# Chunks 0 and 1 of a windowed attention: scores over all 128 rows with zeros beside a head's q, and weighted values over all 128 columns with both heads' v

## The chip, the core and the metric

The kernel runs on one core of one Trainium2 chip. The metric is the device time of one execution in microseconds (us), over a few executions of the same program. Five engines work side by side and wait for one another through semaphores: PE (matrix multiply, with PEld for its weight loads), DVE (vector), ACT (scalar and activation), POOL and SP. SP and ACT also issue the transfers from and to memory. Matmuls read SBUF and write PSUM.

## What is computed

Sliding-window attention with a linear position bias, and behind it a feed-forward layer:

```python
batch, n_heads, seq, head_dim = (8, 8, 576, 64)
...
    window = 128
    scale = 1.0 / np.sqrt(D)
    scores = scale * np.matmul(q, k.transpose(0, 1, 3, 2))
    ...
    bias = slopes[:, None, None] * (-np.abs(rel).astype(np.float32))[None, :, :]
    mask = (rel >= 0) & (rel < window)
    scores = np.where(mask, scores + bias[None], -1000000000.0)
    scores = scores - np.max(scores, axis=-1, keepdims=True)
    attn = np.exp(scores)
    attn = attn / (np.sum(attn, axis=-1, keepdims=True) + 1e-09)
    return np.matmul(attn, v).astype(np.float32)
...
    h = x @ w_in
    g = np.where(pos, h, np.where(neg, 0.0, (h + beta) ** 2 / (4.0 * beta)))
    return (g @ w_out).astype(np.float32)
```

The attention output of 8 heads of 64 makes x of 4608 rows by 512; w_in is 512 by 2048, w_out 2048 by 512. Both weights arrive in 64-bit floats and are converted on the chip.

## The kernel before

**Tiling.** The 4608 tokens are cut into 12 chunks of 384 (`CH`), each of three blocks of 128. A chunk has 8 heads, taken in 4 pairs; the two heads of a pair lie beside each other in the 128 rows of q and k (transposed: row is head dimension, column is token), the even head (j = 0) in rows 0 to 63 and the odd head (j = 1) in rows 64 to 127. Heads are numbered `m` through the whole program (chunk c = m // 8), pairs `p` likewise.

**Stages of a head.** `prepare_q` scales q (L232). `scores` (L264) multiplies, for each of the three blocks, the block's q by up to 256 columns of k into PSUM (tile `s`), DVE adds the bias and takes the row's extremum (L294, tile `z`), ACT exponentiates with a running sum (L296), and DVE divides and folds the two halves of the window into one 128-wide tile `ep` (L302 to L309). `weights_t` (L312) transposes `ep` on PE (L318, tile `p`), ACT copies it out (L321, tile `lu`), and POOL makes a lower and an upper triangle of it (L322, L324). `values` (L337) multiplies v by these triangles into PSUM (tile `x`, L359), and one copy takes the result to `xn`.

**The first two chunks** (`LIGHT = 2`) use plain float32 matmuls, each of which stands in the trace as two PE records; the others use operands split in a high and a low part (L290, L291, L383). In chunks 0 and 1 a score matmul reads the 64 rows of its head alone (`ql[r, 0, qs]`, `kr[r, 0, ks]`, L288), and a value matmul has the 64 columns of its head's v as weights (`vn[:, i + b0, j]`, L359). In chunk 0 the two heads of a pair write the two halves of one PSUM bank, which is copied once for both (L364, DVE for odd pairs, ACT for even ones); in chunk 1 each head has a bank of its own, and is copied alone (L366, L368).

**The feed-forward layer** of a chunk runs over 16 slices of 128 of the inner width (`layer1`, L405 to L419, tiles `h`, `sg`, `g`; `layer2`, L430 to L447, tiles `acc`). Its matmuls are 128 rows by 128 columns: `h` in split form, and in chunk 0 `acc` in plain float32 (L438).

**Order.** Python code writes the attention of chunk c + 1 between the slices of the feed-forward layer of chunk c (`segments`, `emit_attention`). A scheduler then settles each engine's program; an engine runs it strictly in that order. Ahead of the first layer stands the whole attention of chunk 0, and with it the conversion of the first four slices of the weights (`EARLY`, `fetch_weights`, `convert_in`, `convert_out`, L123 to L146) on ACT and DVE; the other twelve are converted during chunk 0's feed-forward layer. Two runs of transposes of the identity (`keep_busy`, L84) stand at the start of PE's program, before and behind the first scores.

Of the kernel before, what the change touches and what calls it, by code (L numbers as in the profile page):

```python
# [8 lines left out]
F32 = mybir.dt.float32  # L9
# [3 lines left out]
AF = mybir.ActivationFunctionType  # L13
# [5 lines left out]
def windowed_attention_then_ffn(  # L19
# [21 lines left out]
    V, S, G, T, DMA = nc.vector, nc.scalar, nc.gpsimd, nc.tensor, nc.sync  # L41

    H, SEQ, D = 8, 576, 64
    NT, DM = out.shape
    DFF = w_in.shape[1]
    P = 128
    NPAIR = H // 2
    NCC = DM // P
    NFC = DFF // P
    NQB = 3  # L50
    CH = NQB * P
# [35 lines left out]

    loaded = const.tile([P, 1], F32, name="loaded")
    S.activation(loaded, quarter, AF.Exp)
    qscale = const.tile([P, NPAIR], F32, name="qscale")  # L90
    for g in range(NPAIR):
        G.memset(qscale[:D, g:g + 1], 4.0 ** g / 4.0)
# [14 lines left out]
    rel_end = const.tile([P, 2 * P], F32, name="rel_end")  # L107
    V.tensor_copy(rel_end, rel)
    V.memset(rel_end[D:, :P + D], NEG)


    wi, wo, wf = [None] * NFC, [None] * NFC, {}
# [68 lines left out]
    def load_first(p):  # L181

        n = f"_{p}"
        if p == 0:
            qq = [ap1.tile([P, CH], F32, name="qr" + n, tag="qr"), ap1.tile([P, 2, CH], F32, name="ql" + n, tag="ql")[:, 0]]
            kv = [ap1.tile([P, CH + P], F32, name="kr" + n, tag="kr")[:, :CH], ap1.tile([P, CH], F32, name="vn" + n, tag="vn")]
        elif p == 1:
            t = ap1.tile([P, 2, CH], F32, name="qq" + n, tag="kl")
            qq = [t[:, 0], t[:, 1]]
            kv = [ap1.tile([P, CH], F32, name="kr" + n, tag="kk"), ap1.tile([P, CH], F32, name="vn" + n, tag="vs")]  # L190
        else:
            t = wp.tile([P, 2, CH], F32, name="qq" + n, tag=f"wi{NFC - NPAIR + p}")
            qq = [t[:, 0], t[:, 1]]
            t = wp.tile([P, 2, CH], F32, name="kv" + n, tag=f"wo{NFC - NPAIR + p}")
            kv = [t[:, 0], t[:, 1]]
        vn = kv[1].rearrange("p (i j d) -> p i j d", j=2, d=D)
        pair[p] = dict(qr=qq[0], ql=qq[1].rearrange("p (o t) -> p o t", o=1), kr=kv[0].rearrange("p (o t) -> p o t", o=1), vn=vn)
        DMA.dma_start(qq[0], q[p * P:(p + 1) * P, :CH])
        DMA.dma_start(kv[0], k[p * P:(p + 1) * P, :CH])
        DMA.dma_start(vn.rearrange("p i j d -> p i (j d)"), v[:CH, p * P:(p + 1) * P].rearrange("(i p) d -> p i d", p=P))  # L200

# [30 lines left out]
    def prepare_q(p):  # L232
        qr = pair[p]["qr"]
        if p // NPAIR < LIGHT:
            if p >= NPAIR:
                pair[p]["ql"] = ap1.tile([P, 2, CH], F32, name=f"ql_{p}", tag="ql")
            return S.activation(pair[p]["ql"][:, 0], qr, AF.Copy, scale=qscale[:, p % NPAIR:p % NPAIR + 1])
        ql = pair[p]["ql"] = ap1.tile([P, 2, CH], F32R, name=f"ql_{p}", tag="ql")
        for j in range(2):
            scale = 2.0 ** (2 * (p % NPAIR) + j + 1) / 8.0  # L240
            o_hi, o_lo, s = ql[lo_rows[j], j], ql[hi_rows[j], j], qr[lo_rows[j]]
            S.mul(o_hi, s, scale)
            V.scalar_tensor_tensor(o_lo, s, scale, o_hi.bitcast(F32), ALU.mult, ALU.subtract)
# [20 lines left out]
    def scores(m, blks):  # L264
# [15 lines left out]
        for n, i in enumerate(blks):  # L280
            lone = i + b0 == 0
            c0 = P if lone else D if c % CYCLE == 1 and i == 2 else 0
            k0 = (i + b0 - 1) * P + c0
            o = pt[:, n, c0:]
            win.append((o, c0, lone))
            if c < LIGHT:
                r, qs, ks = lo_rows[j], slice(i * P, (i + 1) * P), slice(k0, k0 + 2 * P - c0)
                st["scored"] = T.matmul(o, ql[r, 0, qs], kr[r, 0, ks], start=True, stop=True).ins  # L288
                continue
            T.matmul(o, ql[:, j, i * P:(i + 1) * P], kk[:, j, k0:k0 + 2 * P - c0], start=True, stop=False)  # L290
            T.matmul(o, ql[:, j, i * P:(i + 1) * P], kl[:, j, k0:k0 + 2 * P - c0], start=False, stop=True)  # L291
# [45 lines left out]
    def values(m):  # L337
        p, j = divmod(m, 2)
        c, g = divmod(p, NPAIR)
        vn, vs, lu = pair[p]["vn"], pair[p].get("vs"), head[m]["lu"]  # L340
        b0 = before(c)
        if j == 0:
            xn[c, g] = xp1.tile([P, CH], F32, name=f"xn_{c}_{g}", tag=f"xn{g}")
        if c == 0:

            if j == 0:
                pair[p]["px"] = ps_acc.tile([P, DM], F32, name=f"x_{m}", tag="acc")
            pb = pair[p]["px"]
        else:
            pb = bank(f"x_{m}")  # L350
        px, pf = pb[:, :CH], pb.rearrange("r (i w) -> r i w", w=P)
        o = xn[c, g][lo_rows[j]]
        if c < LIGHT:
            po = px[lo_rows[j]] if c == 0 else px[:D]
            todo = [i for i in (0, 1, 2, -1) if i + b0 >= 0]
            for n, i in enumerate(todo):
                q0, q1 = max(i, 0), min(i + 2, NQB)
                first = 2 * i + 1 if i >= 0 else 0
                last_x[0] = T.matmul(po[:, q0 * P:q1 * P], vn[:, i + b0, j],  # L359
                         lu[:, 0, first:first + q1 - q0, :].bitcast(F32).rearrange("p a w -> p (a w)"),  # L360
                         start=(n == 0), stop=(n == len(todo) - 1), skip_group_check=True).ins
            if c == 0:
                if j:
                    (V.tensor_copy if g % 2 else S.copy)(xn[c, g], px)  # L364
            elif j:
                S.copy(o, po)  # L366
            else:
                V.tensor_copy(o, po)  # L368
            del head[m]
            if j == 1:  # L370
                del pair[p]
            return
        alone = -1 if b0 else NQB - 1
        todo = [(i, s) for i in range(-b0, NQB) if i != alone for s in range(2)] + [(alone, 0)]
        for n, (i, s) in enumerate(todo):
            w = vs[:, i + b0, j].rearrange("p s d -> p (s d)")
            q0, q1 = max(i, 0), min(i + 2, NQB)
            first = 2 * i + 1 if i >= 0 else 0
            if i == alone:
                ox, lx = pf[:, q0::NQB - q0, :], lu[:, :, first, :]  # L380
            else:
                ox, lx = px[:, q0 * P:q1 * P], lu[:, s, first:first + q1 - q0, :].rearrange("p a w -> p (a w)")
            T.matmul(ox, w, lx, start=(n == 0), stop=(n == len(todo) - 1), skip_group_check=True)  # L383
        S.copy(o, px[D:, :])
        V.tensor_tensor(o, px[:D, :], o, ALU.add)
        o = o[:, q0 * P:(q0 + 1) * P]
        V.tensor_tensor(o, pf[:D, NQB, :], o, ALU.add)
        del head[m]
        if j == 1:
            del pair[p]  # L390
# [187 lines left out]
```

## Time and profile before

| what | value |
|---|---|
| median of 3 executions | 1060.94 us (1060.28 to 1061.31) |
| the profiled execution's own time | 1068.07 us |
| its span, first to last instruction | 1066.0 us |
| mean granted PE clock | 0.981 |
| PE busy | 97% |
| DVE, ACT, POOL busy | 74%, 58%, 35% |
| first matmul of the first layer | 53.86 us |

The page gives each engine's busy time, then the span in 40 slices (digits are tenths; the row PEclk is the clock that PE was granted), the chain of work that ended last, and the costliest groups of instructions. Other views of the same trace are a table by stretches of time (busy time of each engine, granted clock, transfers), the timeline of one engine, and the chain in order of time. In these, "x6" behind a group of plain float32 matmuls means six records, so three matmuls. PE counts as busy while a matmul is in flight, so 100% does not say that it runs at full clock.

### The profile page before, as it was taken

The numbers are of one execution on the slowest core, as the hardware profiler recorded it, in microseconds if no ns is written. First come the engines' busy times: TensorE is split into PE (matmuls) and PEld (weight loads), VectorE is DVE, ScalarE is ACT, GpSimd is POOL, SyncE is SP. The second block draws the span as 40 slices with busy tenths as digits, with TensorE's granted clock in tenths as the row PEclk, the third lists the DMA queues.
The fourth block names the chain that finished last, engine by engine and source line by source line (L and its number), as shares of the span: only waits on it lengthen the run. The fifth ranks groups of instructions, "written<-read, shape, count | busy, mean of one in ns | idle before, by whom it ended". The sixth has DMA issues, their size and how long they took to land.

```text
span 1066.0 us, 16843 instructions
## 1 busy us (share of the span) xinstructions
PE 1038.2 (97%) x5508; PEld 906.8 (85%) x5508; DVE 790.1 (74%) x2249; ACT 618.9 (58%) x1476; POOL 369.2 (35%) x419
## 2 busy tenths in 40 slices
PE   8999999999999999999999999999999999999998
PEld 5576667998988988998998988999889889899996
DVE  6687799878877788877678887777787897863322
ACT  6687766656556556656456565555555655742322
POOL 2120004444443433433343443433333443333221
PEclk8599999999999999999999999999999999999999
DMA  8346412112212122121113112111121221200000
GB/s 284 100 164 202 136 48 67 53 40 67 65 38 67 48 65 67 41 53 60 36 48 89 43 48 65 62 30 38 60 65 38 77 65 48 67 1 1 31 1 30
DMA packets 58903, 69.50 MB, mean 65 GB/s; under 512 B 4032, under 2 KB 44480, under 8 KB 58816
## 3 DMA queue, kind: packets, MB, share of 16 engines
q1 hardware_dynamic: 48064, 51.66, 17.4%
q10 hardware_dynamic: 10752, 16.78, 4.6%
q8 instruction: 43, 0.70, 0.3%
q14 instruction: 44, 0.36, 0.1%
HBM read 58.98 MB, written 9.44 MB: 64 GB/s over the span
## 4 chain that ended last, share of the span: by engine, by line
PE 85%; DVE 6%; ACT 5%; POOL 2%; issue 2%; DMA 0%; ACTq 0%; SPq 0%; DVEq 0%; POOLq 0%
PE h L408 11%; PE h L409 11%; PE h L410 11%; PE acc L441 11%; PE acc L442 10%; PE acc L443 10%; PE x L383 5%; PE acc L438 3%; PE p L318 3%; PE s L291 2%; PE s L290 2%; PE x L359 2%; PE s L288 2%; ACT z L296 1%; POOL lu L333 1%
## 5 line engine op out<-in xcount | busy, mean ns | idle before, releaser
L427 POOL TENSOR_TENSOR gl<-g,gh 128x384 fp32r<-128x384 f32 x176 | 183.5, 1042 | 435.0 <-ACT gh L426 429.1
L408 PE MATMUL h<-xh,wi 128*128 128x384 f32 x768 | 264.8, 345 | 1.7 <-ACT sg L417 1.7
L409 PE MATMUL h<-xl,wi 128*128 128x384 f32 x768 | 259.8, 338 | 0.0
L410 PE MATMUL h<-xh,wi 128*128 128x384 f32 x768 | 259.4, 338 | 0.0
L441 PE MATMUL acc<-wo,gh 128*128 128x512 f32 x528 | 212.0, 401 | 8.1 <-ACT gh L426 8.1
L418 DVE SCALAR_TENSOR_TENSOR g<-sg 128x384 f32<-128x384 f32 x192 | 108.6, 566 | 148.4 <-ACT sg L417 136.4
L442 PE MATMUL acc<-wo,gh 128*128 128x512 f32 x528 | 208.2, 394 | 0.0
L426 ACT CAST gh<-g 128x384 fp32r<-128x384 f32 x176 | 90.3, 513 | 193.6 <-DVE g L419 179.4
L417 ACT ACTIVATE sg<-h,quarter 128x384 f32<-128x384 f32 x192 | 111.2, 579 | 140.2 <-PE h L410 139.5
L296 ACT ACTIVATE z<-z,nmax 128x256 f32<-128x256 f32 (+2 forms) x288 | 139.0, 485 | 28.5 <-DVE nmax L294 26.6
L443 PE MATMUL acc<-wo,gl 128*128 128x512 f32 x528 | 155.5, 398 | 0.0
L408 PEld LDWEIGHTS h<-xh,wi 128*128 128x128 f32 x768 | 144.6, 188 | 10.7 <-ACT sg L417 3.4
L409 PEld LDWEIGHTS h<-xl,wi 128*128 128x128 f32 x768 | 144.6, 188 | 5.9 <-issue 1.4
L410 PEld LDWEIGHTS h<-xh,wi 128*128 128x128 f32 x768 | 144.4, 188 | 0.0
L294 DVE CUSTOM_DVE_ANT_0 z<-s,rel 128x256 f32<-128x256 f32 (+2 forms) x256 | 94.4, 394 | 51.5 <-PE s L291 44.3
L309 DVE CUSTOM_DVE_ANT_0 ep<-z,rc 128x128 f32<-128x128 f32 x256 | 129.9, 548 | 1.6
L331 POOL TENSOR_SCALAR_AFFINE_SELECT lu<-lu 128x768 fp32r<-128x768 f32 x80 | 80.8, 1010 | 130.2 <-DVE lu L329 121.6
L441 PEld LDWEIGHTS acc<-wo,gh 128*128 128x128 f32 x528 | 99.4, 188 | 27.2 <-ACT gh L426 10.6
L419 DVE SCALAR_TENSOR_TENSOR g<-sg,g 128x384 f32<-128x384 f32 x192 | 112.0, 584 | 3.7
L443 PEld LDWEIGHTS acc<-wo,gl 128*128 128x128 f32 x528 | 97.1, 189 | 19.8 <-POOL gl L427 0.2
L442 PEld LDWEIGHTS acc<-wo,gh 128*128 128x128 f32 x528 | 99.5, 188 | 16.5
L333 POOL TENSOR_SCALAR_AFFINE_SELECT lu<-lu 128x768 fp32r<-128x768 f32 x80 | 81.4, 1018 | 4.6
(88 smaller groups left out, 1461.1 us busy)
## 6 DMA issues: line engine op xcount, KB each, us to landing
kr<-in_k_dram SPq DMA_DIRECT2D x60, 256.0 KB, 4.1
out_dram<-o SPq DMA_DIRECT2D x36, 256.0 KB, 2.4
qr<-in_q_dram SPq DMA_DIRECT2D x45, 192.0 KB, 3.7
rawi<-in_moe_w_in_dram ACTq DMA_DIRECT2D x16, 512.0 KB, 4.6
rawo<-in_moe_w_out_dram ACTq DMA_DIRECT2D x16, 512.0 KB, 5.6
vn<-in_v_dram SPq DMA_DIRECT2D x32, 256.0 KB, 2.8
kr<-in_k_dram SPq DMA_DIRECT2D x26, 192.0 KB, 3.4
vn<-in_v_dram SPq DMA_DIRECT2D x14, 192.0 KB, 2.5
```

The lines of the kernel that those rows point to most:

```text
L296: S.activation(z[:, i, c0:], z[:, i, c0:], AF.Exp, bias=nmax[:, i:i + 1], scale=-1.0, accum_out=sm[:, i, 0:1])
L309: st["folded"] = V.tensor_tensor_reduce(out=ep[:, i, :], in0=z[:, i, :P], in1=z[:, i, P:], op0=ALU.add, op1=ALU.add, scale=rc[:, i:i + 1], ...
L408: T.matmul(ph, wi[fc][:, 0, cc, :], xh, start=(cc == 0), stop=False)
L409: T.matmul(ph, wi[fc][:, 0, cc, :], xl, start=False, stop=False)
L410: T.matmul(ph, wi[fc][:, 1, cc, :], xh, start=False, stop=(cc == NCC - 1))
L417: first = S.activation(sg, ph, AF.Relu, bias=quarter[:, 0:1], scale=0.25)
L418: V.scalar_tensor_tensor(g, sg, 0.5, sg, ALU.min, ALU.mult)
L419: last = V.scalar_tensor_tensor(g, sg, -0.25, g, ALU.add, ALU.max)
L427: G.tensor_tensor(gl, g, gh.bitcast(F32), ALU.subtract)
L441: T.matmul(a, gh[:, ts], wo[fc][:, 0], start=first, stop=False)
L442: T.matmul(a, gh[:, ts], wo[fc][:, 1], start=False, stop=False)
L443: T.matmul(a, gl[:, ts], wo[fc][:, 0], start=False, stop=last)
```

## The change

The edit touches only chunks 0 and 1.

- **Scores.** A tile `qz` holds q of a pair twice, 128 rows by 2 by 384: in plane j only the rows of head j carry q, and the other 64 rows are zero. The score matmul of head j reads all 128 rows of plane j and of k. The zeros are set once: those of `qz[0]` by two fills on DVE, those of the other three tiles by six fills on POOL. Pair 0 and the four pairs of chunk 1 use `qz[0]`, pairs 1 to 3 of chunk 0 the others, which lie in the buffers of weight slices 9 to 11 before these are loaded.
- **q.** `prepare_q` scales each head's 64 rows by an instruction of its own: two on ACT for a pair where there was one.
- **Values.** The weights of a value matmul are both heads' v, 128 columns. Its result has the wanted head in that head's 64 rows, and the product with the other head's v in the others, which nothing reads. In chunk 0 each head now has a PSUM bank of its own, as in chunk 1.
- **Copies out.** Each head's 64 rows are copied alone: j = 0 on DVE, j = 1 on ACT. In chunk 0 that makes eight copies of 64 rows where there were four of 128; in chunk 1 their number and engines stay.

```diff
+    qz = [ap1.tile([P, 2, CH], F32, name=f"qz_{p}", tag="ql") if p == 0 else
+          wp.tile([P, 2, CH], F32, name=f"qz_{p}", tag=f"wi{NFC - 4 - p}") for p in range(NPAIR)]
+    V.memset(qz[0][D:, 0], 0.0)
+    V.memset(qz[0][:D, 1], 0.0)
...
+    for t in qz[1:]:
+        G.memset(t[D:, 0], 0.0)
+        G.memset(t[:D, 1], 0.0)
...
-            qq = [ap1.tile([P, CH], F32, name="qr" + n, tag="qr"), ap1.tile([P, 2, CH], F32, name="ql" + n, tag="ql")[:, 0]]
+            qq = ap1.tile([P, CH], F32, name="qr" + n, tag="qr")
...
-        pair[p] = dict(qr=qq[0], ql=qq[1].rearrange("p (o t) -> p o t", o=1), kr=kv[0].rearrange("p (o t) -> p o t", o=1), vn=vn)
-        DMA.dma_start(qq[0], q[p * P:(p + 1) * P, :CH])
+        pair[p] = dict(qr=qq, ql=qz[p], kr=kv[0].rearrange("p (o t) -> p o t", o=1), vn=vn)
+        DMA.dma_start(qq, q[p * P:(p + 1) * P, :CH])
...
-            if p >= NPAIR:
-                pair[p]["ql"] = ap1.tile([P, 2, CH], F32, name=f"ql_{p}", tag="ql")
-            return S.activation(pair[p]["ql"][:, 0], qr, AF.Copy, scale=qscale[:, p % NPAIR:p % NPAIR + 1])
+            pair[p]["ql"] = qz[p if p < NPAIR else 0]
+            for j in range(2):
+                r = lo_rows[j]
+                o = S.activation(pair[p]["ql"][r, j], qr[r], AF.Copy, scale=qscale[r, p % NPAIR:p % NPAIR + 1])
+            return o
...
-                r, qs, ks = lo_rows[j], slice(i * P, (i + 1) * P), slice(k0, k0 + 2 * P - c0)
-                st["scored"] = T.matmul(o, ql[r, 0, qs], kr[r, 0, ks], start=True, stop=True).ins
+                qs, ks = slice(i * P, (i + 1) * P), slice(k0, k0 + 2 * P - c0)
+
+                st["scored"] = T.matmul(o, ql[:, j, qs], kr[:, 0, ks], start=True, stop=True).ins
...
-            if j == 0:
-                pair[p]["px"] = ps_acc.tile([P, DM], F32, name=f"x_{m}", tag="acc")
-            pb = pair[p]["px"]
+            pb = ps_acc.tile([P, DM], F32, name=f"x_{m}", tag="acc")
...
-                last_x[0] = T.matmul(po[:, q0 * P:q1 * P], vn[:, i + b0, j],
+                last_x[0] = T.matmul(px[:, q0 * P:q1 * P], vn[:, i + b0].rearrange("p j d -> p (j d)"),
...
-            if c == 0:
-                if j:
-                    (V.tensor_copy if g % 2 else S.copy)(xn[c, g], px)
-            elif j:
-                S.copy(o, po)
-            else:
-                V.tensor_copy(o, po)
+            (S.copy if j else V.tensor_copy)(o, px[lo_rows[j]])
```

The scheduler orders the first 200 us or so anew. Three places show it; in the names, the number behind a tile's letter is only its buffer's.

PE, the first values of chunk 0 (`x`, heads 0 and 1), before. The sizes are those of the output.

```order
L288 MATMUL s_0_281<-kr_138,qq_137 128x128
L288 MATMUL s_0_281<-kr_138,qq_137 128x256
L288 MATMUL s_2_288<-kr_138,qq_137 128x256
L359 MATMUL x_274<-lu_221,vn_133 64x256 x2
L359 MATMUL x_274<-lu_221,vn_133 64x128
L359 MATMUL x_274<-lu_253,vn_133 64x256 x2
L359 MATMUL x_274<-lu_253,vn_133 64x128
L318 MATMUL p_300<-ident,ep_233 128x128 x3
```

The same place now:

```order
L298 MATMUL s_0_295<-kr_149,qz_93 128x128
L298 MATMUL s_0_295<-kr_149,qz_93 128x256
L298 MATMUL s_2_302<-kr_149,qz_93 128x256
L367 MATMUL x_287<-lu_234,vn_144 128x256 x2
L367 MATMUL x_287<-lu_234,vn_144 128x128
L328 MATMUL p_315<-ident,ep_246 128x128 x3
L367 MATMUL x_340<-lu_266,vn_144 128x256 x2
L367 MATMUL x_340<-lu_266,vn_144 128x128
```

The two heads' values wrote two halves of one bank one right behind the other; now each writes 128 rows of its own bank, and the transposes of head 2 stand between them.

ACT, from the first q to the exponentials of head 0, before:

```order
L237 ACTIVATE ql_131<-qr_130,qscale 128x384
L133 DMA rawi_154<-in_moe_w_in_dram 128x4x256
L139 DMA rawo_156<-in_moe_w_out_dram 128x1024
L237 ACTIVATE qq_137<-qq_137,qscale 128x384
L296 ACTIVATE z_159,sums<-z_159,nmax_160 128x128
L296 ACTIVATE z_159,sums<-z_159,nmax_160 128x256 x2
```

The same place now:

```order
L245 ACTIVATE qz_92<-qr_142,qscale 64x384 x2
L142 DMA rawi_166<-in_moe_w_in_dram 128x4x256
L148 DMA rawo_168<-in_moe_w_out_dram 128x1024
L245 ACTIVATE qz_93<-qr_148,qscale 64x384 x2
L306 ACTIVATE z_171,sums<-z_171,nmax_172 128x128
L306 ACTIVATE z_171,sums<-z_171,nmax_172 128x256 x2
```

Two instructions of 64 rows stand where one of 128 stood, for pair 0 and for pair 1, and the exponentials of head 0 stand behind both.

POOL, from the table of distances (`reli`, from which `rel`, the bias of every score, is cut) to the first triangle, before:

```order
L97 IOTA reli 128x256
L105 MEMSET sums 128x12
L99 AFFINE_SELECT rel<-rel 128x256
L101 AFFINE_SELECT rel<-rel 128x256
L322 AFFINE_SELECT lu_221<-lu_221 128x3x128
```

The same place now:

```order
L102 IOTA reli 128x256
L110 MEMSET sums 128x12
L117 MEMSET qz_93 64x384
L118 MEMSET qz_93 64x384
L117 MEMSET qz_94 64x384
L118 MEMSET qz_94 64x384
L117 MEMSET qz_95 64x384
L118 MEMSET qz_95 64x384
L104 AFFINE_SELECT rel<-rel 128x256
L106 AFFINE_SELECT rel<-rel 128x256
```

The six fills stand ahead of the two cuts of `rel`, which the first bias on DVE waits for.

More of the change, by code (lines that the diff above doesn't have):

```diff
@@ L184, in load_first @@
         if p == 0:
-            qq = [ap1.tile([P, CH], F32, name="qr" + n, tag="qr"), ap1.tile([P, 2, CH], F32, name="ql" + n, tag="ql")[:, 0]]
+            qq = ap1.tile([P, CH], F32, name="qr" + n, tag="qr")
             kv = [ap1.tile([P, CH + P], F32, name="kr" + n, tag="kr")[:, :CH], ap1.tile([P, CH], F32, name="vn" + n, tag="vn")]
         elif p == 1:
-            t = ap1.tile([P, 2, CH], F32, name="qq" + n, tag="kl")
-            qq = [t[:, 0], t[:, 1]]
+            qq = ap1.tile([P, CH], F32, name="qr" + n, tag="kl")
             kv = [ap1.tile([P, CH], F32, name="kr" + n, tag="kk"), ap1.tile([P, CH], F32, name="vn" + n, tag="vs")]
         else:
-            t = wp.tile([P, 2, CH], F32, name="qq" + n, tag=f"wi{NFC - NPAIR + p}")
-            qq = [t[:, 0], t[:, 1]]
+            qq = wp.tile([P, CH], F32, name="qr" + n, tag=f"wi{NFC - NPAIR + p}")
             t = wp.tile([P, 2, CH], F32, name="kv" + n, tag=f"wo{NFC - NPAIR + p}")
@@ L353, in values @@
         if c < LIGHT:
-            po = px[lo_rows[j]] if c == 0 else px[:D]
             todo = [i for i in (0, 1, 2, -1) if i + b0 >= 0]
```

## The prediction

> **What bounds the kernel now.** I read the page first: the busy times (share of the span, instructions) and the granted clock in 40 slices.
>
> ```profile
> PE 1038.2 (97%) x5508; PEld 906.8 (85%) x5508; DVE 790.1 (74%) x2249; ACT 618.9 (58%) x1476; POOL 369.2 (35%) x419
> PEclk8599999999999999999999999999999999999999
> ```
>
> PE is the bound, 97% busy. The one thing out of line is the digit 5 in the second slice (26.7 to 53.3 us): PE had half its clock there, though that is the attention of chunk 0, with work waiting. So the table by stretches comes next (columns: stretch, length, busy us and count on PE, PEld, DVE, ACT, POOL, granted clock, DMA share, GB/s).
>
> ```profile
> 16.00:20.00 4.00, 4.00 (x18) 2.44 (x18) 3.44 (x18) 2.83 (x10) 0.00 (x0) 0.59 1.05 383
> 20.00:24.00 4.00, 4.00 (x19) 2.36 (x19) 3.11 (x14) 3.93 (x10) 1.04 (x2) 1.00 0.99 305
> 24.00:30.00 6.00, 2.79 (x9) 1.33 (x7) 4.42 (x12) 5.34 (x18) 1.43 (x2) 0.68 0.14 54
> 30.00:40.00 10.00, 9.79 (x26) 6.19 (x27) 7.68 (x37) 6.05 (x19) 2.25 (x5) 0.50 0.46 151
> 40.00:52.50 12.50, 12.50 (x34) 7.28 (x33) 6.49 (x33) 6.49 (x17) 2.47 (x5) 0.50 0.25 69
> 52.50:54.00 1.50, 1.50 (x7) 0.84 (x6) 0.24 (x2) 1.50 (x8) 0.03 (x1) 0.69 0.94 359
> 54.00:74.00 20.00, 19.85 (x90) 13.86 (x91) 16.57 (x63) 16.63 (x42) 3.81 (x9) 1.00 0.46 153
> 74.00:129.00 55.00, 55.00 (x232) 36.74 (x231) 43.15 (x118) 41.16 (x84) 6.77 (x13) 1.00 0.56 183
> 129.00:149.00 20.00, 20.00 (x85) 14.21 (x85) 18.05 (x45) 12.50 (x25) 0.00 (x0) 1.00 0.11 27
> 149.00:178.00 29.00, 25.37 (x126) 20.01 (x125) 28.39 (x71) 21.27 (x51) 10.42 (x9) 1.00 0.31 87
> ```
>
> Four stages with four limits. From 20 to 30 us ACT sets the pace (3.93 of 4, 5.34 of 6). From 30 to 54 PE alone is full, at clock 0.50, while DVE and ACT are about half busy. From 54 to 149 PE is full at clock 1.00. From 149 to 178 DVE is (28.39 of 29). From 40 to 52.5 PE is 100% busy and yet not sped up; from 54 on it is 100% busy and is. What differs is what it runs: before 54, matmuls of 64 rows or 64 columns and some transposes; after it, mostly 128 by 128. PE's timeline (start, us, engine, line, out<-in, rows*columns of the array, count) says the same twice.
>
> ```profile
> 1.65 3.25 PE L84 MATMUL idle<-ident 128*128 128x128 f32 x14 [1.65 <-POOL qscale L92]
> 6.80 2.40 PE L84 MATMUL idle<-ident 128*128 128x128 f32 x20
> 15.98 3.31 PE L359 MATMUL x<-lu,vn 128*64 128x256 f32 x12
> 36.74 2.39 PE L359 MATMUL x<-lu,kv 128*64 128x256 f32 x6
> ```
>
> The first 14 full-width transposes take 0.23 us each, the later 20 take 0.12: full-width work brought the clock up, and it was work on the identity, nearly all zeros. And 12 records of two heads' values in 3.31 us, where 6 of one head take 2.39, means that two halves of the array ran side by side; behind them the clock goes from 0.59 to 1.00. I read from this that the grant follows how much of the array is in use, and that zeros count.
>
> **The change, part by part.** *Clock in 30 to 54 us.* The groups of PE from 30 to 54:
>
> ```profile
> L359 PE MATMUL x<-lu,kv 128*64 128x256 f32 x16 | 7.7, 639 | 0.0
> L318 PE MATMUL p<-ident,ep 128*128 128x128 f32 x15 | 5.0, 446 | 1.3 <-DVE ep L307 1.3
> L288 PE MATMUL s<-kr,ql 64*128 64x256 f32 x8 | 4.1, 671 | 0.0
> L288 PE MATMUL s<-kv,qq 64*128 64x256 f32 x8 | 3.8, 631 | 0.0
> L359 PE MATMUL x<-lu,kv 128*64 128x128 f32 x8 | 2.3, 384 | 0.0
> L288 PE MATMUL s<-kr,ql 64*128 64x192 f32 x4 | 1.7, 524 | 0.0
> L288 PE MATMUL s<-kv,qq 64*128 64x128 f32 x4 | 1.6, 498 | 0.0
> ```
>
> Count times output width is 12,416 columns. The rate at full clock and full width is read from the first layers, in the chain in order of time (start, us, what):
>
> ```profile
> 53.93 0.37 PE h L408
> 76.39 1.38 PE s L288 x6
> 80.08 2.57 PE acc L438 x6
> 82.66 0.33 PE p L318 x3
> 82.98 1.45 PE x L359 x8
> 90.75 0.48 PE p L318 x3
> 123.58 0.37 PE h L408
> 142.97 0.17 PE h L408
> ```
>
> Six `acc` records of 512 columns in 2.57 us are 0.837 ns a column, and `p` with 128-column weights agrees (0.11 us for 128). So PE needs 12,416 x 0.837 ns = 10.4 us where it now takes 23.7 (9.79, 12.50 and the 1.4 up to the first `h` at 53.9). Then ACT and DVE are late next. ACT has 6.05 + 6.49 + 1.5 = 14.0 us of work there, and gets more:
>
> ```profile
> L242 ACT ACTIVATE ql<-qr 64x384 fp32r<-64x384 f32 x2 | 1.0, 522 | 0.0
> L237 ACT ACTIVATE qq<-qq,qscale 128x384 f32<-128x384 f32 x3 | 1.8, 613 | 2.7 <-DMA qq<-in_q_dram 2.7
> L366 ACT COPY xn<-x 64x384 f32<-64x384 f32 x4 | 1.9, 472 | 0.1
> L364 ACT COPY xn<-x 128x384 f32<-128x384 f32 x2 | 1.0, 479 | 3.3 <-PE x L359 3.3
> L368 DVE COPY xn<-x 64x384 f32<-64x384 f32 x4 | 2.2, 541 | 0.0
> ```
>
> 64 rows cost what 128 do (0.472 against 0.479; 0.522 against 0.613), so each second half of a q is about 0.52 us more, and each copy more is 0.47 on ACT or 0.54 on DVE: in all 8 x 0.52 + 2 x 0.47 = 5.1 us on ACT and 2 x 0.54 = 1.1 on DVE. Three q halves and one copy of these fall in this stretch: 14.0 + 2.0 = 16.0 us. DVE has 7.68 + 6.49 + 0.24 + 0.5 = 14.9. The gain is at most 23.7 - 16.0 = 7.7 and at least nothing. ACT where it set the pace was 89% busy (24 to 30 us); at that share 16.0 us of work last 18.0: **-5.7 us**.
>
> *The first 30 us.* Two q halves now stand ahead of head 0's first exponential, and six fills ahead of the cuts of `rel` on POOL:
>
> ```profile
> 7.24 1.47 ACT z L296 x6
> 3.14 0.40 POOL L99 TENSOR_SCALAR_AFFINE_SELECT rel<-rel 128x256 f32<-128x256 f32 x1 [0.35 <-DVE rel L98]
> L300 POOL MEMSET z<- 128x64 f32 x2 | 0.3, 154 | 1.8 <-DVE rc L309 1.8
> masks.py:197 POOL MEMSET ident<- 128x128 f32 x1 | 0.2, 205 | 0.3 <-POOLq L559 0.3
> ```
>
> By 154 and 205 ns for 64 and 128 columns a fill of 384 is 0.41 us, six are 2.5: the cuts start at 5.6 instead of 3.14 and end, at 0.40 each, near 6.5. The first bias, which needs them, goes ahead of the exponential at 7.24, so they cost 0 to 0.9 us, beside the q half's 0.5, which comes at the same moment. The doubled scores and the pair of values at half clock (13.6 to 19.3 us) would save up to 2.5 us at full clock, but ACT sets the pace right behind them and has two more q halves, 1.0 us, to do there. I take **+0.5 us**, with ends at -2.0 and +0.9. DVE's two fills of `qz[0]` stand in time in which DVE waits for `reli`.
>
> *Borders between shapes, 54 to 124 us.* Six `s` records of 1408 columns should take 1.18 us and take 1.38; eight `x` of 1536 should take 1.29 and take 1.45; the first `h` behind either takes 0.37, behind `acc` 0.17; `p` behind `x` takes 0.48, behind `acc` 0.33. So each border between 64 and 128 costs the piece behind it 0.15 to 0.20 us, and `acc` to `h`, which also changes the number format but not the shape, costs nothing. PE's timeline has 30 such borders from the first `h` at 53.9 to that at 123.6: 10 into `h`, 8 into `s`, 8 into `x`, 4 into `p`, in all 2.0 + 1.6 + 1.3 + 0.6 = 5.5 us, on the engine that is full. At full width there are none. Of these, 12 lie before 74, where ACT (16.63 of 20) and DVE are nearly full and ACT gets the last two q halves; I count those at half: **-4.4 us**, with ends at 0 and -5.5.
>
> From 149 on I cost nothing: DVE, full from there to 178, has 3.4 + 11.9 + 2.0 = 17 us of slack from 54 to 149, so it can come there earlier with PE. Without that cover, everything is lost there.
>
> The sum is -5.7 + 0.5 - 4.4 = -9.6 us on the profiled execution's 1068.1, so 1058.5. Its time is 7.1 us above the median of the runs, 1060.9; the difference carries over, and the forecast is **1051.3 us**.
>
> **The rivals.** *B: the clock stays at half.* The rows bear it out as far as 22 us of full PE did not raise it; against it stand the 12 side-by-side records and the identity transposes. PE then needs 12,416 x 1.67 = 20.8 us instead of 23.7 (the borders go), but the pair of values at 16 us, no longer side by side, takes 2 x 2.14 instead of 3.31, 1.0 more: -2.9 + 1.0 + 0.5 - 4.4 = -5.8, **1055.1 us**. The Trainium skill, "TensorE: Matmul & The Clock Gate", Part 1, says that the gate opens after a window of some 3.4 us in which PE is busy; if busy means occupied, width changes nothing and this rival holds, but by that reading the stretch from 40 to 52.5 should already run at 1.00, and its row says 0.50. The same page's Part 3 speaks against the change: matmuls on different strips of the array run concurrently, which full width gives up; the row of 12 in 3.31 us agrees, and the 1.0 us above is its price at half clock.
>
> *C: DVE takes it back.* If DVE cannot come to 149 us earlier, PE waits there for all it gained: **1060.9 us**, give or take 2. For it speaks 28.39 of 29, against it the 17 us of slack.
>
> *D: slower, by ACT's queue.* The 5.1 us of new ACT work lengthen the run where ACT has no idle time left, if also the clock stays and the border cost belongs to the plain float32 weights rather than to shape: +5.1 + 1.0 = **1067.0 us**. It decides once ACT's idle time from 30 to 54 (24 - 14 = 10 us) is under the 2.0 added there. Against it stands that margin, and that `acc`, float32 too, costs no border.
>
> **How the numbers follow.** Forecast 0.62, B 0.21, C 0.10, D 0.07. The best ends (-7.7 - 2.0 - 5.5 = -15.2) give 1045.7; the forecast's poor ends (clock up for half the stretch, -2.9, +0.9, -2.2) 1056.7; B with nothing from 54 to 124 would be 1059.5. The range 1045.5 to 1059 leaves out D and most of C. Within 0.2%, about what a measurement of this kernel can tell from no change, is 1058.8 to 1063.1: C, 0.09. Faster: forecast, B and a little of C, 0.84; slower: 0.07.
>
> **What would show it.** PEclk in the second slice 8 or 9 instead of 5 (B: 5 stays). The first `h` on PE near 48 us instead of 53.9. `s` x6 at 1.18, `x` x8 at 1.29, and `h` behind them at 0.17. ACT some 85 to 90% busy from 30 us to the first `h`. PE's idle time from the first layer's end to 30 us later unchanged at about 3.6 us (C: larger by what was gained). The forecast is wrong if the clock falls back whenever PE, now faster, idles between heads, or if ACT and DVE wait for each other head by head so that the chain and not their work sets that stage.

## The result, and the profile after

| | before | after |
|---|---|---|
| median of 9 executions each | 1060.94 us (1060.28 to 1068.2) | 1055.85 us (1055.16 to 1058.7) |
| ratio | | 0.9943, 95% interval 0.9922 to 0.9965 |
| the profiled execution's own time, mean granted PE clock | 1068.07 us, 0.981 | 1055.43 us, 0.996 |

The kernel became faster by 5.1 us between the medians (0.48%; the ratio, taken over all nine runs of each, is 0.57%): inside the range, 4.5 us above the forecast of 1051.3. Between the two profiled executions the difference is 12.6 us, which is more than the 9.6 forecast for them. Both misses have to be explained.

The page of the changed kernel, its busy times and granted clock in 40 slices:

```profile
PE 1019.9 (97%) x5508; PEld 907.5 (86%) x5508; DVE 792.8 (75%) x2253; ACT 625.7 (59%) x1486; POOL 372.0 (35%) x425
PEclk9999999999999999999999999999999999999999
```

PE runs as many instructions as before (5508) in 18.3 us less, and no slice stands at half clock. The table by stretches (stretch, length, busy us and count on PE, PEld, DVE, ACT, POOL, granted clock, DMA share, GB/s) shows where the time went and what limits now:

```profile
20.00:24.00 4.00, 2.18 (x13) 1.78 (x11) 3.86 (x16) 3.93 (x11) 0.52 (x1) 1.00 1.09 371
24.00:30.00 6.00, 4.09 (x15) 3.33 (x16) 4.26 (x18) 5.93 (x16) 1.27 (x2) 0.76 0.33 102
27.15:30.56 3.41, 3.33 (x13) 2.81 (x12) 2.44 (x14) 3.35 (x10) 0.00 (x0) 0.50 0.26 77
30.56:44.00 13.44, 10.31 (x54) 8.13 (x52) 12.10 (x52) 12.74 (x36) 5.15 (x10) 1.00 0.43 133
44.00:54.00 10.00, 7.38 (x41) 6.24 (x40) 7.47 (x29) 8.44 (x23) 3.29 (x5) 1.00 0.46 164
54.00:74.00 20.00, 20.00 (x92) 15.09 (x91) 18.40 (x65) 18.70 (x42) 3.06 (x7) 1.00 0.59 198
74.00:129.00 55.00, 55.00 (x243) 41.09 (x242) 46.75 (x115) 42.95 (x86) 5.38 (x10) 1.00 0.50 162
136.60:166.60 30.00, 26.73 (x137) 21.49 (x136) 29.53 (x75) 21.24 (x50) 10.07 (x9) 1.00 0.30 84
```

Chunk 0's attention, which PE filled at half clock, is now set by ACT: 5.93 of 6.00 and 12.74 of 13.44 busy, PE idle for a quarter of the time. From 44 to 54 PE, ACT and DVE wait for one another (none is over 85%). From 54 on PE is full, and the stretch that DVE bounds (149 to 178 before) has moved to about 137 to 167, with DVE at 29.53 of 30.

PE's timeline (start, us, engine, line, out<-in, rows*columns, count, idle time before it and what ended that) has the places:

```profile
25.83 1.35 PE L367 MATMUL x<-lu,vn 128*128 128x256 f32 x6 [3.65 <-POOL lu L334]
27.27 0.47 PE L328 MATMUL p<-ident,ep 128*128 128x128 f32 x1
27.53 2.34 PE L298 MATMUL s<-kv,qz 128*128 128x128 f32 x6
35.56 1.35 PE L367 MATMUL x<-lu,kv 128*128 128x256 f32 x6 [1.90 <-POOL lu L334]
44.00 0.42 PE L410 MATMUL h<-xh,wi 128*128 128x384 f32 x1
48.11 0.33 PE L328 MATMUL p<-ident,ep 128*128 128x128 f32 x1 [1.11 <-DVE rc L319]
53.38 0.44 PE L410 MATMUL h<-xh,wi 128*128 128x384 f32 x1 [1.51 <-ACT sg L419]
58.28 1.47 PE L367 MATMUL x<-lu,vn 128*128 128x256 f32 x8
```

The transpose at 27.27, ahead of six `s` records, is the one that stood at 30.21 before: 2.9 us are won by then. The first `h` starts at 44.00 instead of 53.86: 9.9 us. Against before, the twelfth first-layer slice (the `h` at 127.88 before, 116.39 now) is 11.5 us earlier, the sixteenth (148.44 and 136.64) 11.8, and the last of all (1054.15 and 1041.69) 12.5. So four fifths of the difference between the two profiles have arisen by the first `h`, and nothing is lost behind.

### The profile page after: what moved, and what is told of

Its sections match the earlier page's. It is cut to its first block, busy times and chain, and to the rows that moved or that the text cites. A ratio compares the mean times of both kernels' runs of the same rounds, so it can differ in the third digit from the quotient of the medians.

```text
span 1053.6 us, 16864 instructions
## 1 busy us (share of the span) xinstructions
PE 1019.9 (97%) x5508; PEld 907.5 (86%) x5508; DVE 792.8 (75%) x2253; ACT 625.7 (59%) x1486; POOL 372.0 (35%) x425
## 4 chain that ended last, share of the span: by engine, by line
PE 79%; DVE 9%; ACT 7%; issue 3%; POOL 2%; DMA 0%; ACTq 0%; SPq 0%; DVEq 0%; POOLq 0%
PE h L410 11%; PE h L411 11%; PE h L412 11%; PE acc L443 10%; PE acc L444 10%; PE acc L445 10%; PE x L385 5%; PE acc L440 3%; PE p L328 2%; PE s L301 2%; PE s L300 2%; ACT z L306 2%; DVE ep L319 1%; DVE z L304 1%; POOL lu L343 1%
## 5 line engine op out<-in xcount | busy, mean ns | idle before, releaser
L341 POOL TENSOR_SCALAR_AFFINE_SELECT lu<-lu 128x768 fp32r<-128x768 f32 x80 | 80.8, 1010 | 127.3 <-DVE lu L339 117.8
L445 PEld LDWEIGHTS acc<-wo,gl 128*128 128x128 f32 x528 | 97.1, 188 | 19.8
L385 PEld LDWEIGHTS x<-lu,vs 128*128 128x128 f32 x512 | 70.5, 188 | 15.9 <-POOL lu L343 12.2
```

What stands on the lines that cost most here:

```text
L445: T.matmul(a, gl[:, ts], wo[fc][:, 0], start=False, stop=last)
```

## The experiments

Every run has a mean granted PE clock beside its time. The time depends on it: beside the experiments the kernel before ran 88 times (10 as a kernel of its own), from 1059.5 to 1068.3 us, and its 20 runs at a clock of 0.992 have a median of 1060.75, the 14 at 0.981 one of 1067.90. That is 7.15 us for 0.011, or **0.65 us for each 0.001**. 0.001 of a span of 1060 us is 2.1 us at half clock, so a microsecond at half clock costs 0.3. Below, "at a like clock" compares runs of the same mean clock; this is rough, since the mean does not say where in the program the clock was low, and the runs beside 1 to 4, 5 to 8 and 9 to 12 come from three chips. The kernel before's own 11 runs at 0.989 lie between 1061.6 and 1063.5 us, so a difference of a microsecond between a few runs says little.

**1. The kernel before, unchanged.**

> The kernel before, unchanged, profiled and timed again. Theory (the clock's grant in chunk 0's attention differs from run to run, and the profile on which the prediction was made was an unlucky one): the runs spread over several us, the time falls as the granted clock rises, runs near 1061 us have a mean clock near 0.988 to 0.990, runs near 1066 to 1068 have 0.981 to 0.984, and a profile near 1061 shows less than 27 us at half clock before 54 us. Rival (a profiled execution is 7 us longer than a timed one, whatever the clock): all timed runs near 1061 us with the clock at 0.981, and this profile's own time near 1068.

Measured: 1064.73 us (1060.56 to 1068.13), ratio 1.0006 [0.9981, 1.0031]. The profiled execution took 1064.13 us at 0.988, within what the other nine took at their clocks (0.979 to 0.991). It stood at half clock for 17.1 us from 25.7 on, where the first profile did for 27.3 from 26.1; its first `h` started at 48.91 instead of 53.86, 4.95 us earlier, and every later slice up to 576 us by 4.9 to 5.1. Behind one more window of 3.4 us at half clock at 660 us, which the first profile has not, the lead is 3.9 to the end: such a window, where PE is full, costs 1.2. So the 7.1 us that the first profile lay above the median are no cost of profiling: that execution was one of those with the most half clock, and the program itself has no fixed length. Nor does this second profile have the half clock that the first had from 12.5 to 19.3 us.

**2. and 3. One chunk alone.** Chunk 0 alone (scores and values of chunk 1 as before):

```diff
+                if c:
+                    r = lo_rows[j]
+                    st["scored"] = T.matmul(o, ql[r, 0, qs], kr[r, 0, ks], start=True, stop=True).ins
+                    continue
                 st["scored"] = T.matmul(o, ql[:, j, qs], kr[:, 0, ks], start=True, stop=True).ins
...
+                last_x[0] = T.matmul(px[:D, q0 * P:q1 * P] if c else px[:, q0 * P:q1 * P],
+                         vn[:, i + b0, j] if c else vn[:, i + b0].rearrange("p j d -> p (j d)"),
```

> Only chunk 0 has full-width scores and values; chunk 1 is as before. Theory (two separate gains, clock in chunk 0, borders in chunk 1): clock 0.994 to 0.997, the first layer's first matmul near 44 us, time 2 to 4 us under the kernel before, so about 1057.5 to 1058.5. Rival (all of the gain is the clock): the whole 5 us, about 1056.

Chunk 1 alone is the mirror of it, chunk 0 being that of the kernel before.

> Only chunk 1 has full-width scores and values; chunk 0 is as before. Theory: the clock in chunk 0's attention as in the kernel before (mean 0.981 to 0.990, and it may spread), the 30 borders of 0.15 to 0.20 us gone from chunk 0's feed-forward layer, time 2 to 4 us under the kernel before in runs of like clock. Rival (what ACT, DVE and the order do there takes the borders back): within 1 us of the kernel before.

Measured, chunk 0 alone: 1061.65 us (1057.1 to 1065.84), ratio 0.9972 [0.9946, 0.9999], clocks 0.988 to 0.998, the first `h` at 48.36 in its profile: both expectations were missed. At a like clock it is slower than the kernel before: 1061.65 against 1060.75 at 0.992, 1065.22 against 1063.0 at 0.989. Chunk 1 alone: 1056.05 us (1054.43 to 1057.12, four runs), ratio 0.9913 [0.9879, 0.9947], clocks 0.991 to 0.994; at 0.993 it took 1056.05 where the kernel before took 1059.70, so 3.6 us less. What follows, as far as a like mean clock tells: all of the gain at a like clock is chunk 1's, where no border between array shapes is left, and chunk 0's half costs 1 to 2 us; what chunk 0's half gives is clock (0.992 in the mean of these ten runs, 0.988 in the 88).

The trace of chunk 0 alone shows this within one run, in windows of its own:

```profile
25.79:29.20 3.41, 3.41 (x11) 2.95 (x12) 2.18 (x12) 3.36 (x12) 0.00 (x0) 0.50 0.09 36
36.03:39.44 3.41, 3.41 (x11) 2.53 (x10) 1.78 (x10) 1.56 (x4) 0.16 (x1) 0.50 0.14 47
39.44:42.86 3.42, 3.42 (x11) 2.34 (x10) 1.52 (x7) 1.80 (x5) 1.29 (x3) 0.50 0.03 5
46.27:49.68 3.41, 3.41 (x12) 3.05 (x12) 3.06 (x15) 0.90 (x3) 0.16 (x1) 0.50 0.31 95
```

In each of the four PE is busy throughout at half clock. The first holds only full-size matmuls (chunk 0's), and the clock is full behind it. The next two are filled to 57% and 64% by 64-row scores and 64-column values (chunk 1's), and half clock goes on, as it does behind the window from 42.86, with 38%; the last holds only full-size matmuls again, and behind it the clock is full.

**4. Values alone on all columns** (scores, and q in one activation, as before; the copies out as in the changed kernel):

```diff
-            if j == 0:
-                pair[p]["px"] = ps_acc.tile([P, DM], F32, name=f"x_{m}", tag="acc")
-            pb = pair[p]["px"]
+            pb = ps_acc.tile([P, DM], F32, name=f"x_{m}", tag="acc")
...
-                last_x[0] = T.matmul(po[:, q0 * P:q1 * P], vn[:, i + b0, j],
+                last_x[0] = T.matmul(px[:, q0 * P:q1 * P], vn[:, i + b0].rearrange("p j d -> p (j d)"),
```

> Values over all 128 columns in both chunks, scores on a head's 64 rows as before (so no second q halves and no zeros). Theory (the grant follows how much of the array is in use over a few us): full-width values and transposes are enough to lift it, so little time at half clock, mean 0.990 or more; about half of the borders stay; with no second q halves on ACT, which is the bound of chunk 0's attention now, the time is 3 to 6 us under the kernel before. Rival (only all-full-width work lifts the clock): half clock through most of 30 to 50 us, mean 0.981 to 0.988, gain under 2 us.

Measured: 1063.69 us (1060.69 to 1066.2), ratio 0.9992 [0.9971, 1.0012], clocks 0.983 to 0.990: no gain, and a clock as low as before, as the rival had it. Full columns in the values alone do not hold the clock. At a like clock it is 1.0 to 2.2 us under the kernel before (1061.97 against 1063.0 at 0.989, 1063.21 against 1064.97 at 0.987): part of the borders is gone, and ACT has no second q halves.

**5. and 6. Idle transposes in PE's wait**, in the kernel before and in the changed one:

```diff
         emit_attention(turned[m])
+        if t == 4:
+            behind([last_x[0]], lambda: keep_busy(24))
```

> The kernel before, untouched but for 24 idle 128x128 transposes that PE gets behind the values of head 2, where it waits for POOL's triangle from about 24 to 27 us. Theory (the granted clock falls because PE idles in that wait, and half clock costs about 0.3 us per us): no fall at 26 us, mean clock 0.992 to 0.995 in every run, times 1058.5 to 1061, and a median 2 to 4 us under the kernel before of the same call. Rival (64-row scores can't hold the full clock, whatever stands in that wait): the clock falls a few us later all the same, mean clock 0.982 to 0.990 in most runs, 1061 to 1068, the same as before. Second rival (the 2.6 us of transposes end after the triangle is there): +0.5 to +1.5 us at a like clock.

> The changed kernel with the same 24 idle transposes behind the values of head 2. Theory (what is left of its half clock, 3.4 us at 27 us, comes from PE's wait of 3.65 us for POOL's triangle): no half clock after 22 us, mean clock 0.997 or more in every run, times 1054 to 1055.5, the spread of 3.5 us between its runs gone. Rival (the fall is set elsewhere): clock 0.992 to 0.997 and 1055 to 1058.7 as without them. If the transposes outlast the wait: +0.5 us.

Measured, in the kernel before: 1062.71 us (1058.95 to 1073.56), ratio 1.0014 [0.9981, 1.0046], clocks 0.981 to 0.997. In the profiled run (0.997) the half clock from 26 us is gone, as the theory has it, and the time, 1058.95, is lower than any of the 88; but eight of the other nine runs had 0.993 or less, and at a like clock the transposes and the order that the scheduler made around them cost 2 us and more (1062.71 against 1060.75 at 0.992, one run of 1073.56 against 1067.90 at 0.981). In the changed kernel: 1057.69 us (1053.97 to 1060.17), ratio 0.9943 [0.9919, 0.9968]; three runs at 0.998 took 1054.0 to 1054.5, the other seven 1056.2 to 1060.2 at 0.992 to 0.994. Its profile still has a stretch of half clock, at 31.5 us, behind the next wait. So in these profiles PE's wait goes with the fall of the clock, but there is more than one such wait, and filling one only moved the fall in the second. The theories' medians were missed; the rivals came nearer.

**7. q in two activations of 64 rows**, all else as before:

```diff
-            return S.activation(pair[p]["ql"][:, 0], qr, AF.Copy, scale=qscale[:, p % NPAIR:p % NPAIR + 1])
+            for r in lo_rows:
+                o = S.activation(pair[p]["ql"][r, 0], qr[r], AF.Copy, scale=qscale[r, p % NPAIR:p % NPAIR + 1])
+            return o
```

> The kernel before, with each pair's scaled q of chunks 0 and 1 written in two 64-row activations in place of one of 128 rows; matmuls, copies and layout as before. Theory (the about 2 us at a like clock that chunk 0 alone cost over the kernel before are ACT's extra activations): 1.0 to 2.0 us above the kernel before at a like clock (1060.5 to 1061.5 at 0.993, 1064 to 1065 at 0.989). Rival (they come from the separate banks and copies of the values, or from the order): at a like clock within 0.5 us of the kernel before (1059.5 at 0.993, 1063.1 at 0.989).

Measured: 1067.15 us (1062.18 to 1072.26), ratio 1.0033 [1.0007, 1.006], clocks 0.978 to 0.991. At a like clock 0.2 us above the kernel before at 0.988, 0.5 at 0.987, 1.2 at 0.990, 1.6 at 0.991 and 3.5 at 0.986: above it throughout, but scattered over the theory and the rival both. What was not expected is that the clock falls too. The edit alone costs 4 us at the median (0.33% by the ratio).

**8. and 12. The q halves of pairs 2 to 7 on POOL**, in the changed kernel, twice:

```diff
-                o = S.activation(pair[p]["ql"][r, j], qr[r], AF.Copy, scale=qscale[r, p % NPAIR:p % NPAIR + 1])
+                if p < 2:
+                    o = S.activation(pair[p]["ql"][r, j], qr[r], AF.Copy, scale=qscale[r, p % NPAIR:p % NPAIR + 1])
+                else:
+                    o = G.tensor_scalar(pair[p]["ql"][r, j], qr[r], 4.0 ** (p % NPAIR) * (0.5 if j else 0.25), None, ALU.mult)
...
-        behind(done_t[2 * p - 3][1:2] if 2 <= p <= NPAIR + 1 else [], lambda: prepare_q(p))
+        behind(done_t[2 * p - 3][2:3] if 2 <= p < 2 * NPAIR else [], lambda: prepare_q(p))
```

> The changed kernel with the q halves of pairs 2 to 7 written by POOL, each behind the triangles of the head that it stood behind on ACT; those of pairs 0 and 1 stay on ACT. Theory (ACT bounds chunk 0's attention, 97% busy from 16 to 48 us): four activations of 0.47 us leave its queue ahead of the first h, which starts at about 42.5 instead of 44.0, and the time is 1053.5 to 1055. Rival (POOL's triangles are what heads wait for, and the scaling delays them or lengthens the q's own wait): 1056 to 1058, the first h at 44 or later. If both engines are tied head by head: 1055 to 1056.

> The changed kernel with the q halves of pairs 2 to 7 on POOL again, beside the changed kernel. Theory (the 3 us that it was faster than the changed kernel at a clock of 0.992, 1055.3 to 1055.7 against 1058.7, are ACT's four activations in chunk 0 and those of chunk 1): 1053.5 to 1056, and 2 to 3 us under the changed kernel at any like clock; at 0.995 or more 1053 to 1054.5. Rival (like clocks by the span's mean hide where the falls lie, and the two are the same): within 1 us of the changed kernel's median and of its times at a like clock.

Measured: 1055.55 us (1054.46 to 1055.72), ratio 0.9920 [0.9890, 0.9951], and 1055.02 us (1054.3 to 1055.91), ratio 0.9927 [0.9902, 0.9952]. The groups of POOL and the timeline of PE in the first of them:

```profile
L248 POOL TENSOR_SCALAR qz<-qr 64x384 f32<-64x384 f32 x10 | 13.4, 1341 | 0.6
```

```profile
42.52 0.42 PE L413 MATMUL h<-xh,wi 128*128 128x384 f32 x1
```

A half takes POOL 1.34 us, over twice what ACT needs, and still the first `h` starts at 42.5, as expected, because ACT was what chunk 0 waited for. The first set's median lies just above the 1053.5 to 1055 of the theory. At a like clock of 0.992 the two sets took 1055.34 (5 runs) where the changed kernel took 1058.55 (2 runs), at 0.995 1054.46 (5) against 1056.11 (2). But the medians are within 1 us of the changed kernel's: part of it went back in clock. The same trace, far behind:

```profile
316.40:320.95 4.55, 2.05 (x13) 1.53 (x11) 4.36 (x8) 3.53 (x11) 2.66 (x2) 1.00 0.18 38
320.95:324.36 3.41, 2.92 (x10) 2.54 (x11) 3.38 (x14) 1.55 (x5) 1.15 (x2) 0.50 1.02 358
324.36:327.78 3.42, 3.42 (x21) 3.24 (x20) 2.60 (x9) 1.72 (x6) 1.13 (x1) 1.00 0.16 40
```

PE is busy for 2.05 of 4.55 us, then has half clock for 3.41, then full clock again. In the changed kernel's two profiles the clock did not fall there. Faster than the changed kernel by more than the intervals it is not.

**9. The changed kernel again**, beside 10, 11 and 12.

> The changed kernel again, beside the kernel before and the three below. Theory (its gain is about 5 us of clock and about 1 us at a like clock): median 1055 to 1057, mean clock 0.992 to 0.997, ratio 0.992 to 0.996. Rival (the gain was a draw of clocks that another set would not repeat): median 1058 or more with clocks under 0.992 in half of the runs.

Measured: 1055.73 us (1055.41 to 1058.4), ratio 0.9942 [0.9924, 0.996], clocks 0.992 to 0.997, as in the first set. The gain was no draw.

**10. Scores alone on all rows**, with the values on 64 columns as before:

```diff
-                last_x[0] = T.matmul(px[:, q0 * P:q1 * P], vn[:, i + b0].rearrange("p j d -> p (j d)"),
+                last_x[0] = T.matmul(po[:, q0 * P:q1 * P], vn[:, i + b0, j],
```

> Chunks 0 and 1 with scores on all rows and q halves as in the changed kernel, but the values on 64 columns as before. Theory (it is work that fills rows and columns alike that lets the clock stay full, and the borders are gone only where scores and values both have one shape): mean clock 0.984 to 0.990, a median of 1061 to 1066, and at a like clock 1 to 2 us above the kernel before (q halves, no border gone). Rival (rows alone do it, since values alone did not): mean clock 0.992 to 0.997, median 1056 to 1060.

Measured: 1062.82 us (1058.91 to 1064.21), ratio 0.9998 [0.9976, 1.002], nine runs at 0.988 to 0.990 and one at 0.997. As with the values alone, the half measure gives nothing; at a like clock it is within a microsecond of the kernel before (1062.45 against 1063.0 at 0.989, or against 1061.8 in the same set), not 1 to 2 us above it.

**11. Chunk 1 alone with its q halves on POOL**, the edit of 8 applied to the kernel of 3.

> Chunk 0 as in the kernel before; chunk 1 on the full array as in the changed kernel, with its q halves written by POOL behind the triangles. Theory (chunk 1's borders are worth 3.6 us at a like clock, and ACT's four q halves cost chunk 1 up to 1.5 us of it): 1053 to 1056, 1 to 2 us under the 1056.05 that chunk 1 alone gave with its q halves on ACT, 4 to 5 us under the kernel before at a like clock. Rival (in chunk 1 the q halves lie in ACT's idle time): 1055.5 to 1057, nothing gained.

Measured: 1060.78 us (1057.24 to 1062.47), ratio 0.9974 [0.9954, 0.9993], clocks 0.984 to 0.991. At a like clock it is 3.9 us under the kernel before at 0.989, 4.4 at 0.987 and 5.4 at 0.985, as expected, but the clock was as low as in the kernel before, which has the same chunk 0, so the 1053 to 1056 of the theory was missed. The one run at 0.991 took 1057.24, that of experiment 3 at 0.991 took 1057.12: by these two single runs nothing is gained over ACT, the rival. It also warns of experiment 3: its four runs had clocks that ten runs of a kernel with the same chunk 0 hardly reached, so its median of 1056.05 may be a lucky draw.

The clock by kernel: where all of chunk 0 was on the full array, the mean over the runs was 0.995 (changed kernel, 19 runs), 0.995 (6), 0.993 (8 and 12) and 0.992 (2); where it was not, 0.988 (kernel before, 88 runs), 0.986 (4), 0.990 (5), 0.986 (7), 0.990 (10), 0.987 (11), and 0.993 in the four runs of 3.

## Why the prediction was right, and where it was not

**The forecast's mechanisms are the ones that acted**; two terms came out larger between the two profiles, partly because the first profile of the kernel before was of an execution with much half clock, and the last step, from the profiled execution to the median, failed. The time alone would not have shown the mechanism: 1055.85 lies 0.75 us from rival B's 1055.1 and 4.5 from the forecast. What decides against B is the granted clock in the traces.

*Clock in 30 to 54 us, forecast -5.7.* From the transpose to the first `h` it was 30.21 to 53.86 before, 23.65 us, and is 27.27 to 44.00 now, 16.73: **-6.9**. In the second profile of the kernel before the stretch takes 20.68 us (28.23 to 48.91), so against that execution the term is -4.0. The limit behind PE is ACT, as reckoned (rival B has fallen: half clock is 3.4 us long instead of 27.3). ACT is busier there than the 89% assumed, 95%. A q half costs it more than the 0.52 us of the sum, which was read from an activation that takes no `qscale`:

```profile
L245 ACT ACTIVATE qz<-qr,qscale 64x384 f32<-64x384 f32 x13 | 7.9, 608 | 2.0 <-DMA qr<-in_q_dram 1.8
```

At 0.61 us a half, the eight halves and two copies are 5.8 us instead of 5.1. The page's sign, a digit of 8 or 9 in the second slice, is there; the first `h` was forecast near 48 and came at 44.0, since the first 30 us gave more as well.

*The first 30 us, forecast +0.5.* The two parts came as forecast. In the chain in order of time and in POOL's timeline of the changed kernel:

```profile
7.72 1.49 ACT z L306 x6
```

```profile
5.68 0.40 POOL L104 TENSOR_SCALAR_AFFINE_SELECT rel<-rel 128x256 f32<-128x256 f32 x1
```

Head 0's exponentials start at 7.72 instead of 7.24, and the cuts of `rel` at 5.68, where 5.6 was forecast. But the term was **-2.9** by the transpose at 27.27: the half clock from 12.5 to 19.3 did not happen, and what it saved was not eaten by ACT behind it. That was the end of -2.0 that the prediction named and did not take. But most of it is not shown to be the change's doing. The transpose in the two profiles of the kernel before, then in the second of the changed kernel:

```profile
30.21 0.48 PE L318 MATMUL p<-ident,ep 128*128 128x128 f32 x1 [1.25 <-DVE ep L307]
```

```profile
28.23 0.48 PE L318 MATMUL p<-ident,ep 128*128 128x128 f32 x1 [1.25 <-DVE ep L307]
```

```profile
28.42 0.42 PE L328 MATMUL p<-ident,ep 128*128 128x128 f32 x1
```

The unchanged kernel, in an execution without that half clock, is there at 28.23, 2.0 us earlier; against it the changed kernel won 1.0 in one profile and lost 0.2 in the other. The half clock at 12 to 14 us stands in five of the eight profiles with half-size work in chunk 0 and in none of the six without, so the change seems to make it rarer.

*Borders, forecast -4.4 (of 5.5).* The chain of the changed kernel in order of time, in the first layer:

```profile
58.45 1.31 PE x L367 x8
59.76 0.22 PE p L328 x2
59.98 1.19 PE s L298 x6
61.17 0.17 PE h L410
...
66.18 1.31 PE x L367 x8
67.49 0.86 PE s L298 x4
68.36 0.18 PE h L410
```

1.31, 1.19 and 0.17 where 1.45, 1.38 and 0.37 stood; 1.29, 1.18 and 0.17 were forecast. With these, the 30 borders (three of them between 64 rows and 64 columns, the others between 64 and 128) are worth 10 x 0.20 + 8 x 0.19 + 8 x 0.14 + 4 x 0.15 = 5.2 us. From the first `h` to the sixteenth only 1.9 of them arrived, because PE, now ahead, waits 2.6 us from 44 to 54 (10.00 - 7.38): 1.51 for ACT's `sg` and 1.11 for DVE's fold. The prediction had put a discount of half on the borders before 74; the waits took more. Experiments 3 and 11 have chunk 1's half by itself (borders, q halves and new order together), with chunk 0 as before: 3.3 to 5.4 us at a like clock. In the profile of 3 the first `h` to the sixteenth takes 91.1 us (47.38 to 138.48), where both profiles of the kernel before have 94.6: 3.5 us won there.

*149 to 178 us, forecast nothing.* The stretch begins 11.8 us earlier, and PE's idle time in it is 3.27 of 30 us (136.6 to 166.6) where it was 3.63 of 29: rival C has fallen, DVE's slack ahead of it sufficed. *Rival D* has fallen as a whole; but its mechanism, new work in ACT's queue, is real, and the sum paid too little for it: at a like clock chunk 0 alone costs 1 to 2 us, q in two activations 0.2 to 3.5, and with six pairs' halves taken off ACT the changed kernel wins 1.7 to 3.2. The profiles show where: the first `h` to the sixteenth takes 94.6 us in the kernel before, 96.9 with chunk 0 alone (48.36 to 145.29) and 97.1 with q in two activations (50.69 to 147.82). In experiment 2 no q of chunk 1 is split, so whether ACT's instructions or the scheduler's new order cost it there is not shown.

*The step that failed* is "the difference carries over". The sum was made against an execution at 0.981, and 5.7 of its 9.6 us were the price of half clock in that execution. The median of 1060.9 is that of runs at 0.992 (20 such runs of the 88 have 1060.75). A mean clock of 0.981 is about 40 us at half clock ((1 - 0.981) x 2 x 1066), one of 0.992 about 17. The median run had less than half of that clock to win. By the measured slope, from 0.992 to 0.996 there were 4 x 0.65 = 2.6 us, and at a like clock of 0.992 the changed kernel is 2.2 us under the kernel before: together 4.8, against 5.1 measured. That the forecast's sign and range held rests on the borders and on the bounds; its central number was that of the wrong execution.

*"Wrong if the clock falls back whenever PE, now faster, idles between heads":* it does at times (27.15 and 904 us in one profile, 25.96 and 36.2 in the other), but there, behind full-size work, it came back after one window of 3.4 us.

## What to carry to other kernels

List the granted clock of every run before working a profile's time over to a median: where the profiled execution's clock is not that of the median runs, a term that removes half clock counts only for the half clock which those runs have. Where the clock is down, work that leaves half of the array idle is dear beyond its own duration, since a full window of it mostly leaves the clock where it was, and zeros that fill the array were enough to bring it back. Price the instructions that such filling adds on the engine that is next in line, and try them on an idle engine even at twice the duration (1.7 to 3.2 us at a like clock here, nothing beyond the intervals at the median), and look whether the new order gives the full engine a new wait.

## What was not expected of the hardware

In all fourteen traces the changes of the granted clock lie whole multiples of 3.413 us apart. Cutting each trace from some 9 us on into these windows, without the last ones, in which the program ends, and with PE's busy share from its records:

| window | followed by full clock |
|---|---|
| half clock, PE busy for 90% or more, only matmuls on 128 rows and 128 columns of the array | 27 of 27 |
| half clock, busy for 90% or more, 30% or more of it matmuls of 64 rows or 64 columns | 11 of 36 |
| half clock, busy for less than 90%, at most 8% of the window such matmuls | 2 of 9 |
| half clock, busy for less than 90%, 30% or more of it as above | 0 of 9 |
| full clock, busy for 46% or less | 0 of 20 |
| full clock, busy for 47 to 57% | 7 of 23 |

The other four falls of the forty came at 12 to 14 us, behind windows busy for 81 to 89%, with 64-row matmuls in 45 to 58% of the busy time; two such windows in the profiles of 1 and 3 were followed by full clock. The kernel before has such a wait at 24 us and then eight windows at half clock, with half-size work in 65% or more of each. Its rows, the window of the fall's cause, the first at half clock, the last one, and the one behind:

```profile
22.72:26.13 3.41, 1.68 (x8) 0.79 (x7) 3.41 (x10) 3.41 (x11) 1.04 (x2) 1.00 0.64 229
26.13:29.54 3.41, 2.39 (x6) 1.20 (x6) 1.90 (x5) 2.80 (x10) 0.39 (x1) 0.50 0.00 0
50.03:53.44 3.41, 3.41 (x11) 1.94 (x10) 2.00 (x4) 3.41 (x10) 0.75 (x1) 0.50 1.00 312
53.44:56.86 3.42, 3.42 (x18) 2.73 (x17) 2.82 (x12) 1.50 (x5) 1.20 (x3) 1.00 0.24 89
```

Where the windows lie against the program differs from execution to execution (the half clock after the wait starts at 27.15 in one profile of the changed kernel and at 25.96 in the other), which fits the spread of one and the same program from 1059.5 to 1068.3 us. The Trainium skill, "TensorE: Matmul & The Clock Gate", Part 1, has the gate open after a window of some 3.4 us in which PE is busy and close after an idle one, with windows that run free of the kernel's start. The windows' length and their free phase agree with these traces; but PE busy with half-size matmuls was followed by full clock in 11 windows of 36 only, and half clock followed windows that were far from idle, 16 of the 23 that were busy for 47 to 57%: there the measurement decides. What exactly is counted, rows, columns or both, and with what threshold, stays open: 64-column matmuls with full rows and 64-row ones with full columns (experiments 10 and 4) both left the clock at 0.983 to 0.990 in all runs but one, and no experiment varied the share in steps.
